# The transformed tokens of two batches in one ring buffer instead of one buffer per batch

## Chip, cores and metric

One core of a Trainium2 chip (trn2). The metric is the device time of one execution in microseconds; lower is better. The tables give medians.

## The reference

A global filter along the sequence, then a feed-forward layer with exact Gelu. There are 8 batches of 3008 tokens of width 256, and the feed-forward layer is 2048 wide.

```python
X = np.fft.rfft(x, axis=1)                          # x: (8, 3008, 256)
Y = X * (filt_r + 1j * filt_i)[None]
t = np.fft.irfft(Y, n=3008, axis=1).reshape(24064, 256)
h = t @ w_in                                        # (24064, 2048)
out = (0.5 * h * (1 + erf(h / sqrt(2)))) @ w_out    # (24064, 256)
```

## The kernel before

The transform is done in four stages of matmuls. The last of them, `s4`, leaves the tokens of one batch transposed in SBUF, in a tile `y` of its own (two such tiles in turn). The feed-forward part walks over all 24,064 tokens in 47 chunks of 512, whatever batch they belong to. As 3008 is not a multiple of 512, a chunk can hold the end of one batch and the start of the next. `segs` then cuts it in two, and each piece needs its own matmul and its own weight load.

```python
def s4(self, b, grp, half, both=False):
    if grp == 0 and half == 0:
        self.y[b] = self.py.tile([128, 2, 3072], BF16, tag="y", name="y_sb")   # py: 2 buffers
    # ... four matmuls into ps ...                                  (L306)
    self._evac(yv, pv, both, 1.0 / self.S)     # into y[b]: L221 on DVE, some L217 on ACT

def segs(self, t):
    lo, hi, r = t * TCH, (t + 1) * TCH, []
    while lo < hi:
        b = lo // self.S
        n = min(hi, (b + 1) * self.S) - lo
        r.append((b, lo - b * self.S, n))
        lo += n
    return r

def mm1(self, t, jc):                          # one of 16 blocks of 128 columns of w_in
    # ...
    for b, off, n in self.segs(t):
        for dc in range(2):
            nc.tensor.matmul(ps[:, o:o + n], lhsT=self.w_in_sb[:, dc, jc * 128:jc * 128 + 128],
                             rhs=self.y[b][:, dc, off:off + n], ...)             # L407
        o += n
    nc.scalar.activation(out=self.st["g", t][:, jc, :], in_=ps, func=AF.Gelu)   # L410
```

The stages of the next batch are mixed into the feed-forward part slot by slot. A slot is one `mm1` of a chunk (two matmuls of 512 columns) and one `mm2` of the chunk before it (four matmuls of 256 columns, L421). `hi` is the first slot of the chunk in which the next batch begins:

```python
s1, n1, r1, s2, n2, r2, s4, n4 = hi - 94, 1, hi - 78, hi - 69, 3.7, hi - 23, hi - 17, 1
# s1: first stage (L232). r2: read back of the third stage's result from DRAM into d_sb. s4: last stage (L306)
```

So the reads of `d_sb` are issued 6 slots before the first L306 that needs them.

## Time and profile before

| | before |
|---|---|
| median of the 6 runs beside the changed kernel | 793.72 us (793.10 to 794.52) |
| the profiled run | 792.14 us, span 790.4 us |
| PE busy | 96% of the span, 90% of the chain that ended last |
| weight loads of the first matmul (L407) | 1728, of which 224 from split chunks |

In the profile's lines PE is TensorE with its matmuls, PEld the loading of TensorE's weights, ACT ScalarE, DVE VectorE and POOL GpSimd; L407 is line 407 of the kernel, and `ps_h<-y_sb,w_in_sb` says which tile is written from which.

The main lines of the page are in the prediction below. Two views more, of the kernel before: the waits of PE, and the waits of PE's weight loads. The columns are the line that waited, what for, the sum in us, how many times, and the longest.

```profile
PE ps_c L322 <- DMA x_sb<-in_x_dram: 10.3, 4, 6.2
...
PE ps_s L306 <- DMA d_sb<-R: 2.0, 5, 0.8
```

```profile
PEld L306 <- DMA d_sb<-R: 2.9, 4, 1.3
...
PEld L306 <- issue: 2.1, 3, 0.8
```

The matmul and its weight load wait side by side, so the two sums overlap and must not be added. PE waits for DMA at the start (x, and then the filters, which show in the chain), and now and then for `d_sb` before the last transform stage.

### The profile page before, as it was taken

To read this page: it belongs to the slowest core of one execution; us is meant where nothing else is said; L and a number is where in the kernel's file an instruction comes from. 1 tells how busy PE (TensorE), PEld (TensorE's weight loads), DVE (VectorE), ACT (ScalarE), POOL (GpSimd) and SP (SyncE) were. 2 spreads that over 40 slices of the span, in tenths; PEclk is the share of its full clock that TensorE was granted. 3 is DMA by queue.
4 is the path that set the end of the run, shared out by engine and by line. 5 is a ranking of instruction groups with operands and counts; after the bars stand their busy time and mean duration, and the time that the engine had idled before them with its cause. 6 is when DMAs were issued, how large, how long until landed. Compare 5 with 4: busy or idle time off the path is not lost.

```text
span 790.4 us, 14879 instructions
## 1 busy us (share of the span) xinstructions
PE 762.5 (96%) x5950; PEld 545.3 (69%) x6042; DVE 407.4 (52%) x733; ACT 570.1 (72%) x982; POOL 65.3 (8%) x161
## 2 busy tenths in 40 slices
PE   4799999999999999999999999999999999999997
PEld 4656776666676767767677677777767676676666
DVE  7794766466463645646455564536545376411011
ACT  6688965798557985588755887568965788566663
POOL 8610200011000100002000010001100000000000
PEclk9999999999999999999999999999999999999999
DMA  8994862565434653446614466154642521501111
GB/s 125 187 163 134 152 157 68 147 123 117 107 87 153 107 136 88 105 136 132 147 45 120 140 116 158 48 170 94 130 121 74 154 80 54 134 31 37 41 41 54
DMA packets 88390, 87.23 MB, mean 110 GB/s; under 512 B 6080, under 2 KB 78272, under 8 KB 88320
## 3 DMA queue, kind: packets, MB, share of 16 engines
q1 hardware_dynamic: 77760, 68.70, 30.6%
q0 software_dynamic: 10560, 17.57, 15.6%
q8 instruction: 47, 0.77, 0.4%
q14 instruction: 23, 0.19, 0.1%
HBM read 57.15 MB, written 46.66 MB: 131 GB/s over the span
## 4 chain that ended last, share of the span: by engine, by line
PE 90%; DMA 4%; POOL 2%; DVE 2%; issue 1%; ACT 0%; SPq 0%; DVEq 0%; POOLq 0%
PE ps_o L421 41%; PE ps_h L407 37%; PE ps_s L232 3%; PE ps_s L306 3%; PE ps_s L279 2%; PE ps_s L255 2%; DMA d_sb<-R 2%; DMA F<-in_filt_i_dram 1%; POOL F L95 1%; DMA x_sb<-in_x_dram 1%; DVE d_sb L219 1%; POOL x_sb L87 1%; DVE p L352 0%; DVE y_sb L221 0%; POOL kap L457 0%
## 5 line engine op out<-in xcount | busy, mean ns | idle before, releaser
L410 ACT ACTIVATE g_sb<-ps_h 128x512 bf16<-128x512 f32 x752 | 439.1, 596 | 190.2 <-PE ps_h L407 166.0
L421 PE MATMUL ps_o<-w_out_sb,g_sb 128*128 128x256 bf16 x3008 | 449.1, 272 | 2.6
L407 PE MATMUL ps_h<-y_sb,w_in_sb 128*128 128x512 bf16 (+7 forms) x1636 | 428.1, 350 | 0.2 <-ACT y_sb L217 0.2
L421 PEld LDWEIGHTS <-g_sb 128*128 128x128 bf16 x3008 | 287.7, 98 | 128.3
L407 PEld LDWEIGHTS <-w_in_sb 128*128 128x128 bf16 x1728 | 164.9, 98 | 27.1 <-issue 0.5
L425 DVE COPY ost<-ps_o 128x512 f32<-128x512 f32 x94 | 64.4, 685 | 125.2 <-PE ps_o L421 124.7
L262 DVE TENSOR_TENSOR p<-ps_s,F 128x512 bf16<-128x512 f32 x84 | 58.1, 692 | 103.5 <-ACT p L261 97.0
L221 DVE TENSOR_SCALAR y_sb<-ps_s 128x376 bf16<-128x376 f32 x120 | 65.3, 548 | 82.4 <-PE ps_s L306 82.4
L219 DVE CAST a_sb<-ps_s 96x512 bf16<-96x512 f32 x112 | 76.3, 686 | 41.0 <-PE ps_s L232 40.9
L219 DVE CAST v_sb<-ps_s 128x512 bf16<-128x512 f32 x84 | 57.6, 687 | 12.9 <-PE ps_s L279 12.9
L306 PEld LDWEIGHTS <-d_sb 96*128 96x128 bf16 x512 | 33.8, 97 | 30.7 <-DMA d_sb<-R 2.9
L260 ACT ACTIVATE p<-ps_s 64x512 bf16<-64x512 f32 x84 | 49.8, 593 | 2.1 <-ACT g_sb L410 0.2
L261 ACT CAST p<-ps_s 64x512 bf16<-64x512 f32 x84 | 48.5, 577 | 1.0
L100 POOL COPY gate<-p 1x1 bf16<-1x1 bf16 x48 | 8.5, 176 | 479.8 <-DVE p L264 479.8
L232 PE MATMUL ps_s<-x_sb,T 94*96 94x512 bf16 x112 | 42.9, 383 | 0.4
L306 PE MATMUL ps_s<-T,d_sb 96*128 96x94 bf16 x448 | 36.3, 204 | 3.1 <-DMA d_sb<-R 2.0
L264 DVE TENSOR_TENSOR p<-p,p 128x512 bf16<-128x512 bf16 x84 | 35.7, 425 | 2.9
L87 POOL DMA_DIRECT2D x_sb<-in_x_dram x64 | 33.9, 530 | 19.3 <-issue 11.0
L263 DVE TENSOR_TENSOR p<-p,F 128x512 bf16<-128x512 bf16 x84 | 34.9, 415 | 0.0
L279 PE MATMUL ps_s<-p,T 128*128 128x256 bf16 x168 | 32.1, 273 | 0.4
L255 PE MATMUL ps_s<-b_sb,T 128*128 128x256 bf16 x168 | 32.1, 273 | 0.4
L279 PEld LDWEIGHTS <-T 128*128 128x128 bf16 x168 | 16.4, 98 | 20.0 <-DVE p L264 0.5
(84 smaller groups left out, 188.4 us busy)
## 6 DMA issues: line engine op xcount, KB each, us to landing
out_dram<-ost SPq DMA_DIRECT2D x94, 256.0 KB, 2.6
x_sb<-in_x_dram POOLq DMA_DIRECT2D x64, 188.0 KB, 4.0
R<-a_sb SPq DMA_DIRECT2D x56, 192.0 KB, 3.0
b_sb<-R SPq DMA_DIRECT2D x28, 384.0 KB, 4.3
R<-v_sb SPq DMA_DIRECT2D x42, 256.0 KB, 4.0
d_sb<-R SPq DMA_DIRECT2D x56, 192.0 KB, 4.5
w_in_sb<-in_moe_w_in_dram POOLq DMA_DIRECT2D x2, 512.0 KB, 8.9
w_out_sb<-in_moe_w_out_dram POOLq DMA_DIRECT2D x2, 512.0 KB, 9.6
```

Source lines behind the costliest of these rows:

```text
L219: self.nc.vector.tensor_copy(out=out, in_=in_)
L221: self.nc.vector.tensor_scalar(out=out, in0=in_, scalar1=scale, scalar2=None, op0=ALU.mult)
L232: nc.tensor.matmul(ps[0:96, :], lhsT=self.T1, rhs=self.st[b, "x"][:, 2 * u:2 * u + 2, :], start=True, stop=True)
L260: nc.scalar.activation(out=p2[0:64], in_=ps[64:128], func=AF.Copy, scale=-1.0)
L261: nc.scalar.copy(out=p2[64:128], in_=ps[0:64])
L262: nc.vector.tensor_tensor(out=p1, in0=ps, in1=f(0), op=ALU.mult)
L279: nc.tensor.matmul(ps[:, 256 * i:256 * i + 256], lhsT=self.T3[:, k].rearrange("p a b -> p (a b)"), rhs=w[:, 256 * i:256 * i + 256], start= ...
L306: nc.tensor.matmul(ps[:, 94 * i:94 * i + 94], lhsT=d[:, (grp % 2) * 4 + i, 128 * half:128 * half + 128], rhs=t4, start=True, stop=True)
L407: nc.tensor.matmul(ps[:, o:o + n], lhsT=self.w_in_sb[:, dc, jc * 128:jc * 128 + 128], rhs=self.y[b][:, dc, off:off + n], start=(dc == 0), ...
L410: nc.scalar.activation(out=self.st["g", t][:, jc, :], in_=ps, func=AF.Gelu)
L421: nc.tensor.matmul(ps[:, tile_i % 2, :], lhsT=g[:, jc, tile_i * 128:tile_i * 128 + 128], rhs=self.w_out_sb[:, jc, :], start=(jc == 0), sto ...
L425: nc.vector.tensor_copy(out=ost, in_=ps)
```

## The change

Its intent: boundaries between batches 0|1, 2|3, 4|5 and 6|7 no longer split a chunk, because two batches lie one behind the other in one buffer of 6016 tokens. Only the boundaries where the ring wraps (batches 2, 4 and 6) still do. The three scratch arrays of the table set-up share that one buffer before the tokens need it.

```diff
--- before.py
+++ after.py
@@ -48,7 +48,7 @@
         self.pd = pool("pd", 4)
         self.pool = pool
         self.po = pool("po", 3)
-        self.py = pool("py", 2)
+        self.py = pool("py", 1)
         self.pg = pool("pg", 2)
         self.small = pool("small", 1)
         self.dram = pool("dram", 2, space=bass.MemoryType.DRAM)
@@ -156,8 +156,7 @@
         v.tensor_copy(out=ri, in_=ri_i)
         ts(out=n2, in0=n2, scalar1=1.0 / self.S, scalar2=None, op0=ALU.mult)
         ts(out=ri, in0=ri, scalar1=-0.25, scalar2=0.25, op0=ALU.mult, op1=ALU.add)
-        wr = self.py.tile([128, 2, K1, NB], FP32, tag="y", name="wr")
-        w, r = wr[:, 0], wr[:, 1]
+        w, r = self.gen[:, 1], self.gen[:, 2]
         ts(out=w, in0=self.kap, scalar1=n2, scalar2=ri, op0=ALU.mult, op1=ALU.add)
         ts(out=r, in0=w, scalar1=RND, scalar2=-RND, op0=ALU.add, op1=ALU.add)
         v.tensor_tensor(out=w, in0=w, in1=r, op=ALU.subtract)
@@ -296,9 +295,10 @@
 
     def s4(self, b, grp, half, both=False):
         nc = self.nc
-        if grp == 0 and half == 0:
-            self.y[b] = self.py.tile([128, 2, 3072], BF16, tag="y", name="y_sb")
-        y = self.y[b]
+        if b == 0 and grp == 0 and half == 0:
+
+            self.ring = self.py.tile([128, 2, 2 * self.S], BF16, tag="y", name="y_sb")
+        o = b % 2 * self.S
         d = self.st[b, "d", grp // 2]
         ps = self.bank("ps_s4", both)
         t4 = (self.T4 if b else self.T4c).rearrange("p a b -> p (a b)")
@@ -306,7 +306,7 @@
             nc.tensor.matmul(ps[:, 94 * i:94 * i + 94],
                              lhsT=d[:, (grp % 2) * 4 + i, 128 * half:128 * half + 128],
                              rhs=t4, start=True, stop=True)
-        yv = y[:, half, 0:self.S].rearrange("c (m w) -> c m w", w=HB)[:, :, 4 * grp:4 * grp + 4]
+        yv = self.ring[:, half, o:o + self.S].rearrange("c (m w) -> c m w", w=HB)[:, :, 4 * grp:4 * grp + 4]
         pv = ps[:, 0:376].rearrange("c (i m) -> c m i", i=4)
         self._evac(yv, pv, both, 1.0 / self.S)
 
@@ -388,11 +388,10 @@
 
 
     def segs(self, t):
-        lo, hi, r = t * TCH, (t + 1) * TCH, []
+        lo, hi, r, m = t * TCH, (t + 1) * TCH, [], 2 * self.S
         while lo < hi:
-            b = lo // self.S
-            n = min(hi, (b + 1) * self.S) - lo
-            r.append((b, lo - b * self.S, n))
+            n = min(hi, (lo // m + 1) * m) - lo
+            r.append((lo % m, n))
             lo += n
         return r
 
@@ -402,10 +401,10 @@
             self.st["g", t] = self.pg.tile([128, 16, TCH], BF16, tag="g", name="g_sb")
         ps = self.ps_h.tile([128, TCH], FP32, tag="h", name="ps_h")
         o = 0
-        for b, off, n in self.segs(t):
+        for off, n in self.segs(t):
             for dc in range(2):
                 nc.tensor.matmul(ps[:, o:o + n], lhsT=self.w_in_sb[:, dc, jc * 128:jc * 128 + 128],
-                                 rhs=self.y[b][:, dc, off:off + n], start=(dc == 0), stop=(dc == 1))
+                                 rhs=self.ring[:, dc, off:off + n], start=(dc == 0), stop=(dc == 1))
             o += n
         nc.scalar.activation(out=self.st["g", t][:, jc, :], in_=ps, func=AF.Gelu)
 
@@ -452,7 +451,8 @@
                           in_=m.T1.rearrange("p (h r k) -> p k h r", h=2, r=2))
     m.load_x(0, 1, 2)
     m.pi = m.iota(g, "pi", [128, 1], [[0, 1]], cm=1, dt=I32)
-    m.kap = m.py.tile([128, K1, 2 * NB], FP32, tag="y", name="kap")[:, :, 0:NB]
+    m.gen = m.py.tile([128, 3, K1, NB], FP32, tag="y", name="gen")
+    m.kap = m.gen[:, 0]
     for sgn, lo in ((1, 0), (-1, 32)):
         nc.gpsimd.iota(m.kap[:, :, lo:lo + 32], pattern=[[1, K1], [sgn * NA, 32]], base=min(0, sgn * NA),
                        channel_multiplier=0, allow_small_or_imprecise_dtypes=True)
```

## The prediction

> **What bounds the kernel now.** I read the page first: the busy shares, then the chain that ended last, then the costly groups.
>
> ```profile
> PE 762.5 (96%) x5950; PEld 545.3 (69%) x6042; DVE 407.4 (52%) x733; ACT 570.1 (72%) x982; POOL 65.3 (8%) x161
> ...
> PE 90%; DMA 4%; POOL 2%; DVE 2%; issue 1%; ACT 0%; SPq 0%; DVEq 0%; POOLq 0%
> ...
> L421 PE MATMUL ps_o<-w_out_sb,g_sb 128*128 128x256 bf16 x3008 | 449.1, 272 | 2.6
> L407 PE MATMUL ps_h<-y_sb,w_in_sb 128*128 128x512 bf16 (+7 forms) x1636 | 428.1, 350 | 0.2 <-ACT y_sb L217 0.2
> L421 PEld LDWEIGHTS <-g_sb 128*128 128x128 bf16 x3008 | 287.7, 98 | 128.3
> L407 PEld LDWEIGHTS <-w_in_sb 128*128 128x128 bf16 x1728 | 164.9, 98 | 27.1 <-issue 0.5
> ```
>
> PE is busy 96% of the span and is 90% of the chain, so whatever leaves PE's queue should shorten the time, one for one. The change touches only the first matmul of the feed-forward part (L407). Its weight loads are 1728. Without splits there would be 47 chunks x 16 column blocks x 2 halves of the depth = 1504. The other 224 are 7 batch boundaries x 32. (Of the matmuls themselves only 1636 records are left in the trace, so I count by the loads.)
>
> The mean durations are a trap. In the groups kept apart by shape, a 512-column matmul of L407 is 379 ns, a 448-column one 353 and a 64-column one 193. So a pair of pieces seems to cost 167 ns more than a whole. But consecutive matmuls overlap, and these ends are modelled. What counts is the spacing of starts. I therefore looked at the timeline of ACT, where one Gelu (L410) marks each slot (one slot is two first matmuls and four second ones of 256 columns, plus what is mixed in). Four stretches: chunk 41, split 64/448 with nothing mixed in; chunk 42, not split, nothing mixed in; chunk 5, split 448/64 with one transform matmul (L232) per slot; chunk 17, split 320/192, also with L232. In each line the first number is the start.
>
> ```profile
> 703.79 0.60 ACT L410 ACTIVATE g_sb<-ps_h 128x512 bf16<-128x512 f32 x1 [0.28 <-PE ps_h L407]
> 704.66 0.60 ACT L410 ACTIVATE g_sb<-ps_h 128x512 bf16<-128x512 f32 x1 [0.28 <-PE ps_h L407]
> 705.54 0.60 ACT L410 ACTIVATE g_sb<-ps_h 128x512 bf16<-128x512 f32 x1 [0.28 <-PE ps_h L407]
> 706.41 0.60 ACT L410 ACTIVATE g_sb<-ps_h 128x512 bf16<-128x512 f32 x1 [0.28 <-PE ps_h L407]
> ```
>
> ```profile
> 717.72 0.60 ACT L410 ACTIVATE g_sb<-ps_h 128x512 bf16<-128x512 f32 x1 [0.27 <-PE ps_h L407]
> 718.59 0.60 ACT L410 ACTIVATE g_sb<-ps_h 128x512 bf16<-128x512 f32 x1 [0.27 <-PE ps_h L407]
> 719.45 0.60 ACT L410 ACTIVATE g_sb<-ps_h 128x512 bf16<-128x512 f32 x1 [0.27 <-PE ps_h L407]
> 720.32 0.60 ACT L410 ACTIVATE g_sb<-ps_h 128x512 bf16<-128x512 f32 x1 [0.27 <-PE ps_h L407]
> ```
>
> ```profile
> 129.59 0.60 ACT L410 ACTIVATE g_sb<-ps_h 128x512 bf16<-128x512 f32 x1 [0.51 <-PE ps_h L407]
> 130.69 0.60 ACT L410 ACTIVATE g_sb<-ps_h 128x512 bf16<-128x512 f32 x1 [0.51 <-PE ps_h L407]
> 131.80 0.60 ACT L410 ACTIVATE g_sb<-ps_h 128x512 bf16<-128x512 f32 x1 [0.51 <-PE ps_h L407]
> 132.91 0.60 ACT L410 ACTIVATE g_sb<-ps_h 128x512 bf16<-128x512 f32 x1 [0.51 <-PE ps_h L407]
> ```
>
> ```profile
> 324.91 0.60 ACT L410 ACTIVATE g_sb<-ps_h 128x512 bf16<-128x512 f32 x1 [0.50 <-PE ps_h L407]
> 326.00 0.60 ACT L410 ACTIVATE g_sb<-ps_h 128x512 bf16<-128x512 f32 x1 [0.50 <-PE ps_h L407]
> ```
>
> The split slot of chunk 41 takes about 0.873 us and the whole slot of chunk 42 about 0.868. ACT waits for PE ahead of every Gelu, so this spacing is PE's. With the trace's nanoseconds averaged over 14 slots: chunk 41 873.5, chunk 42 868.5, chunk 5 1106.7, chunk 17 1093.5.
>
> **What the Trainium skill says.** "TensorE: Matmul & The Clock Gate", section "Back-to-back issue gap", gives for the full clock N/2.4 + 2.5 ns between starts: 215.8 ns for 512 columns, 109.2 for 256, with the 2.5 ns a fixed cost per matmul. A slot of two and four comes to 868.3; the trace has 868.5. By the same formula a split adds two fixed costs, 5.0 ns a slot; chunk 41 shows 5.0. The same section also gives a sustained 131 ns per 512-column matmul in streams of loads and matmuls; this trace doesn't have that. The section "LDWEIGHTS (loading the stationary operand)" puts a load at its columns over 1.2 GHz, 107 ns for 128; the trace has 98. If loads were not hidden, chunk 41 would have shown two loads more per slot, about 196 ns; it shows 5. The page "Perfetto Trace Analysis", section "Identifying the Most-Contended Engine", warns that matmul busy time is a poor measure because matmuls are pipelined; the 379 ns durations against 216 ns spacings agree.
>
> **The change part by part.**
> First, splits removed. The ring holds two batches, 6016 tokens, so only boundaries 2, 4 and 6 remain split. Boundaries 1, 3, 5 and 7 lie in chunks 5, 17, 29 and 41 and become whole: 4 x 32 = 128 matmuls and 128 loads less. The order of the built program agrees: 12,086 rows on PE before, 11,830 after.
> - Chunk 41: 16 slots x 5.0 ns = 0.08 us (its 16 slots took 13.968 us, those of chunk 42 13.893: 0.075).
> - Chunks 17 and 29: a transform matmul is mixed in. Its slot cost comes from chunk 0, where a slot is two first matmuls and one L232: 651.8 ns; less 2 x 215.8 that leaves 220. So an unsplit slot with it is 868.5 + 220 = 1088.5 and the split one 1093.5: again 5.0. Two chunks x 16 x 5.0 = 0.16 us.
> - Chunk 5: 1106.7 - 1088.5 = 18 ns a slot, in 14 slots. The reason may be that two short matmuls of 64 columns come last and the load for L232 behind them (123 ns, 94 rows by 96 columns, against 98 for the usual one) isn't hidden under them. Chunk 41, where the short pieces come first and an L421 load follows long ones, has no such excess. 14 x 18 + 2 x 5 = 0.26 us.
> Sum: 0.08 + 0.16 + 0.26 = 0.50 us, all on PE and on the path.
>
> Second, waits moved. A joined chunk reads both batches in one matmul, so it has to wait for the last write of the new batch before its first matmul, where before the old batch's piece could start without it. In the built program the wait for DVE stands on the first LDWEIGHTS of these four chunks. In the trace before, the last L221 write of batch 1 ends 1.03 us ahead of the first load of chunk 5; for the batches 3, 5 and 7 it is 1.32 us. So this wait costs nothing, unless DVE is pushed back by a microsecond.
>
> Third, the table work at the start. The three scratch arrays move into one tile, and the frequencies become contiguous. L161 read them with gaps in 1.08 us, against 0.96 us for the similar L162 without: 0.1 us at best on DVE. But there the chain is the loads of x and of the filters (DMA of the filters and its issue on POOL are the largest part of the chain in the first 50 us). 0 us. The instruction counts of DVE, ACT, POOL and SP are unchanged, and so is what is transferred.
>
> **The rivals.**
> A: one tile for two batches makes false dependences. If a read of the old batch waited for each write of the new one, each of the 16 slots with an L306 group would hold PE for an eviction, some 0.55 us (L221: 548 ns each) and a hop. 7 batches x 16 x 0.5 us = 56 us, over 840 us in all. In favour: there is one buffer where two were. Against: in the built program L407 has the same 750 waits for ACT, and 15 for DVE before and after (four now on a LDWEIGHTS), so the dependences are kept by range and none was added. The evictions of L221 carry only their 120 waits for PE in both. I hold this at about 1%.
>
> B: the busy durations are real costs. 128 loads x 98 ns = 12.5 us, or 32 x (167 + 166 + 166 + 167) ns = 21 us from the durations of the shapes; the time would be 773 to 781, and the larger one just over 2% faster. In favour: PE is the bound and its busy time will fall by that much. Against: chunks 41 and 42 differ by 0.075 us, where this would want 3 to 5. About 1%.
>
> C: the gain drowns in waits that vary. In the last slot before the L306 groups start, the chunks 9, 15, 21, 27, 33 and 39 stretch to between 1.04 and 2.01 us, waiting for the second transform's reads back from DRAM (d_sb). Over the smallest, 1.04, that is 2.8 us in sum in this one run, from 0 to 0.97 each. It differs from batch to batch with the same program, so it will differ from run to run, and by more than 0.5 us. The three runs before span 1.36 us. This is my main case for the size of the visible difference: the traces may differ by 0.5 us plus or minus 1.
>
> **Range and chances.** 793.73 - 0.50 = 793.2 us. The uncertainty is that of rival C: about 0.8 us either way for a median of a few runs, some more if the layout shifts DMA phases. I take 792.0 to 794.5. Faster by over 2% would need rival B, slower by over 2% rival A: 1% each. 98% within 2%.
>
> **What would show it right or wrong.** L407 should have 1600 weight loads, and no shapes of 448 or 64 columns; 192 and 320 columns also vanish, while 384/128 and 256 stay. The Gelu starts of chunk 41 should come every 0.8685 us, those of chunk 17 every 1.0885 and of chunk 5 every 1.0885 (1.107 before); chunks 11, 23 and 35 keep 1.0935. PE busy time should fall by more than the span does, since the modelled durations overlap. L407 should show no wait for DVE at the head of chunks 5, 17, 29 and 41. The remaining difference in span should lie in the waits for d_sb. I would be wrong if a wait of L407 for y appeared with several hundred ns a time, if the start of the first L407 (49.2 us) moved by more than a microsecond, or if the chunks that were joined shortened by 2 us or more each.

## The result and the profile after

| | before | changed |
|---|---|---|
| median of 6 runs | 793.72 us (793.10 to 794.52) | 791.91 us (790.64 to 793.63) |
| ratio | | 0.9978, 95% interval 0.9965 to 0.9991 |
| span of the profiled run | 790.4 us | 790.6 us |

Within 2%, as forecast, but 0.1 us under the lower end of the range of 792.0 to 794.5, and the difference of 1.8 us is more than three times the 0.5 us forecast. And yet the span of the profiled run is 0.2 us longer, not shorter. So the two traces cannot show a gain of 1.8 us; they show what a single run is made of. In the changed kernel most lines bear a number one lower: L407, L410, L421 and L232 of before are L406, L409, L420 and L231 (L306 stays). First the page of the changed kernel, beside the lines that the prediction quotes of before:

```profile
PE 762.5 (96%) x5817; PEld 539.1 (68%) x5914; DVE 407.6 (52%) x733; ACT 570.5 (72%) x982; POOL 65.3 (8%) x161
...
L406 PE MATMUL ps_h<-y_sb,w_in_sb 128*128 128x512 bf16 (+2 forms) x1503 | 426.6, 365 | 0.2 <-ACT y_sb L216 0.2
L406 PEld LDWEIGHTS <-w_in_sb 128*128 128x128 bf16 x1600 | 155.1, 98 | 23.0 <-issue 0.5
```

The loads of the first matmul (now L406) fell from 1728 to 1600 and their busy time by 9.8 us, while PE's busy time stayed at 762.5. Almost 10 us of this line's weight-load time left the trace and PE is as busy as before.

Then the slots. In the timeline of ACT each Gelu (now L409) marks one slot of PE, and the first column is its start. Chunk 41 of the changed kernel, whole now:

```profile
704.06 0.60 ACT L409 ACTIVATE g_sb<-ps_h 128x512 bf16<-128x512 f32 x1 [0.27 <-PE ps_h L406]
704.93 0.60 ACT L409 ACTIVATE g_sb<-ps_h 128x512 bf16<-128x512 f32 x1 [0.27 <-PE ps_h L406]
705.80 0.60 ACT L409 ACTIVATE g_sb<-ps_h 128x512 bf16<-128x512 f32 x1 [0.27 <-PE ps_h L406]
706.66 0.60 ACT L409 ACTIVATE g_sb<-ps_h 128x512 bf16<-128x512 f32 x1 [0.27 <-PE ps_h L406]
```

And chunk 5, whole now, with the first transform stage mixed in:

```profile
130.38 0.60 ACT L409 ACTIVATE g_sb<-ps_h 128x512 bf16<-128x512 f32 x1 [0.49 <-PE ps_h L406]
131.47 0.60 ACT L409 ACTIVATE g_sb<-ps_h 128x512 bf16<-128x512 f32 x1 [0.49 <-PE ps_s L231]
132.56 0.60 ACT L409 ACTIVATE g_sb<-ps_h 128x512 bf16<-128x512 f32 x1 [0.49 <-PE ps_h L406]
133.65 0.60 ACT L409 ACTIVATE g_sb<-ps_h 128x512 bf16<-128x512 f32 x1 [0.49 <-PE ps_h L406]
```

The spacing in chunk 41 went from 0.873 to 0.868 us, that in chunk 5 from 1.107 to 1.09. From the trace's nanoseconds, averaged over 14 slots: chunk 41 from 873.4 to 868.4, chunks 17 and 29 from 1093.3 to 1088.4, chunk 5 from 1106.6 to 1088.4. The waits of the changed kernel for the reads back:

```profile
PE ps_s L306 <- DMA d_sb<-R: 1.3, 3, 0.6
```

```profile
PEld L306 <- DMA d_sb<-R: 2.3, 3, 1.0
```

To see the whole, I split each trace by the first Gelu of each chunk. (The time of a chunk is from its first Gelu to the first Gelu of the next. The six chunks "before L306" are 9, 15, 21, 27, 33 and 39, whose last slot waits for the first reads of `d_sb`.)

| us | before | changed | difference |
|---|---|---|---|
| from the start to the first Gelu | 49.90 | 50.85 | +0.96 |
| chunks 5, 17, 29, 41 (the joined ones) | 65.96 | 65.47 | -0.49 |
| the six chunks before L306 | 89.22 | 88.84 | -0.38 |
| the other 37 chunks | 585.29 | 585.44 | +0.15 |
| span | 790.36 | 790.60 | +0.24 |

The joined chunks show the forecast: 17.459, 17.269, 17.268 and 13.968 us became 17.193, 17.193, 17.194 and 13.893. The rest is in places that the change doesn't touch. The start came 0.96 us later, where the chain goes through the loads of x and the filters. Single chunks before L306 moved from -0.72 (chunk 39) to +0.65 us (chunk 27) with nothing changed in their programs.

So the question for the experiments: is the missing 1.3 us of the timed gain (1.8 - 0.5) chance in these DMA waits, or something that the new layout brings and that a single pair of traces can't show?

- **Theory N:** the change is worth the 0.5 us in four chunks, and the rest is noise, of the before side too.
- **Theory L:** the layout (ring, merged scratch) systematically shortens the start or the DMA waits by a microsecond.
- **Theory S:** the splits themselves were worth 1.8 us and the trace misleads.

### The profile page after: what moved, and what is told of

The parts are those of the page before. It is cut to its first block, busy times and chain, and to the rows that moved or that the text cites. A ratio compares the mean times of both kernels' runs of the same rounds, so it can differ in the third digit from the quotient of the medians.

```text
span 790.6 us, 14618 instructions
## 1 busy us (share of the span) xinstructions
PE 762.5 (96%) x5817; PEld 539.1 (68%) x5914; DVE 407.6 (52%) x733; ACT 570.5 (72%) x982; POOL 65.3 (8%) x161
## 4 chain that ended last, share of the span: by engine, by line
PE 90%; DMA 5%; DVE 2%; POOL 1%; issue 1%; ACT 0%; SPq 0%; DVEq 0%; POOLq 0%
PE ps_o L420 41%; PE ps_h L406 37%; PE ps_s L231 3%; PE ps_s L306 3%; PE ps_s L278 2%; PE ps_s L254 2%; DMA d_sb<-R 1%; DMA F<-in_filt_i_dram 1%; DMA F<-in_filt_r_dram 1%; DMA x_sb<-in_x_dram 1%; DVE d_sb L218 1%; POOL x_sb L87 1%; POOL F L95 1%; DMA R<-a_sb 1%; DMA b_sb<-R 0%
## 5 line engine op out<-in xcount | busy, mean ns | idle before, releaser
L409 ACT ACTIVATE g_sb<-ps_h 128x512 bf16<-128x512 f32 x752 | 439.4, 597 | 189.1 <-PE ps_h L406 163.5
L420 PE MATMUL ps_o<-w_out_sb,g_sb 128*128 128x256 bf16 x3008 | 449.0, 272 | 3.0
L406 PE MATMUL ps_h<-y_sb,w_in_sb 128*128 128x512 bf16 (+2 forms) x1503 | 426.6, 365 | 0.2 <-ACT y_sb L216 0.2
L420 PEld LDWEIGHTS <-g_sb 128*128 128x128 bf16 x3008 | 287.6, 98 | 133.7
L406 PEld LDWEIGHTS <-w_in_sb 128*128 128x128 bf16 x1600 | 155.1, 98 | 23.0 <-issue 0.5
L306 PEld LDWEIGHTS <-d_sb 96*128 96x128 bf16 x512 | 33.8, 97 | 30.2 <-issue 2.3
L259 ACT ACTIVATE p<-ps_s 64x512 bf16<-64x512 f32 x84 | 49.9, 594 | 2.2 <-ACT g_sb L409 0.2
L231 PE MATMUL ps_s<-x_sb,T 94*96 94x512 bf16 x112 | 42.6, 381 | 0.5
L306 PE MATMUL ps_s<-T,d_sb 96*128 96x94 bf16 x448 | 36.3, 204 | 2.6 <-DMA d_sb<-R 1.3
```

What stands on the lines that cost most here:

```text
L231: nc.tensor.matmul(ps[0:96, :], lhsT=self.T1, rhs=self.st[b, "x"][:, 2 * u:2 * u + 2, :], start=True, stop=True)
L259: nc.scalar.activation(out=p2[0:64], in_=ps[64:128], func=AF.Copy, scale=-1.0)
L306: nc.tensor.matmul(ps[:, 94 * i:94 * i + 94], lhsT=d[:, (grp % 2) * 4 + i, 128 * half:128 * half + 128], rhs=t4, start=True, stop=True)
L420: nc.tensor.matmul(ps[:, tile_i % 2, :], lhsT=g[:, jc, tile_i * 128:tile_i * 128 + 128], rhs=self.w_out_sb[:, jc, :], start=(jc == 0), sto ...
```

## Experiments

### The kernel before against itself, and the changed kernel again

No edit in either. The kernel before stood at 792.12 us (11 runs, 790.80 to 793.98).

> The kernel before, unchanged, timed against itself: how far two equal kernels come apart. Theory N (the change is worth the 0.5 us of PE work of the four joined chunks, and the other 1.2 us of the measured 1.8 is chance in the DMA waits): ratio within 0.9985 to 1.0015, and the intervals of such comparisons wide enough for 1 us. Theory L (the new layout itself brings more than a microsecond): this run shows a ratio within 0.9995 to 1.0005, noise too small for the missing 1.2 us.

Measured: 793.43 us, ratio **1.0012** (0.9998 to 1.0027), between equal programs. Its span is 1.67 us longer than in the first trace of the same kernel; the first Gelu alone came 1.94 us later (51.84 instead of 49.90 us). The joined chunks are 65.965 us against 65.964. Theory L's bound for the noise (0.9995 to 1.0005) was missed: 0.9 us between equal kernels is possible with this many runs.

> The changed kernel again. Theory N: the ratio moves towards 0.9994 (0.5 us), anywhere in 0.998 to 1.0005. Theory L: 0.9978 again, within 0.0007. Both: in its trace the chunks 5, 17, 29 and 41 take 17.19, 17.19, 17.19 and 13.89 us, as in the first trace of it; all other differences from the trace before lie at the first L406 and in the chunks that wait for the reads back (9, 15, 21, 27, 33, 39).

Measured: 791.75 us, ratio **0.9994** (0.9980 to 1.0008). In the trace the four chunks take 17.194, 17.194, 17.193 and 13.893 us. The changed kernel hardly moved from the first measurement (791.91); it is the kernel before that came out 1.6 us lower than before (792.12 after 793.72). That suggests that most of the first difference was on the before side, but doesn't prove it: `before_again`, the same program in the same rounds, stood at 793.43. Theory N's band holds the ratio; theory L's 0.9978 lies just outside the interval. Pooled (12 changed runs against 23 of the kernel before), the difference of the means is -1.1 us plus or minus 0.7, which holds the forecast 0.5. My expectation on where differences lie was not complete: chunk 4, before the L306 of batch 1, was off by 0.34 us too, with a wait of the same kind.

### The ring with all boundaries split

```diff
-            n = min(hi, (lo // m + 1) * m) - lo
+            n = min(hi, (lo // self.S + 1) * self.S) - lo
```

The layout of the change with PE's instructions of before.

> The ring and the merged scratch of the change, but each batch boundary still split, so PE has all the matmuls of before. Theory N: ratio 1.000 within the noise (0.9985 to 1.0015). Theory L: 0.9984, 1.3 us faster than before, as only the 0.5 us of the matmuls is given up. Theory S (the splits alone were worth 1.8 us, the trace misleads): 1.000, while the changed kernel of the same rounds is at 0.9978.

Measured: 792.75 us, ratio **1.0007** (0.9992 to 1.0022). Theory L's 0.9984 is outside the interval. At most some 0.6 us of gain is left to the ring (the lower end of the interval, 0.9992). The four boundary chunks are 65.962 us, as in the kernel before: the ring alone removes nothing there. The six chunks before L306 do not settle it: they take 89.22 and 88.97 us in the two traces of the kernel before, and 88.84, 88.07 and 87.89 us in the three with the ring (`after`, `after_again` and this run). They are shorter in all three, but that is three traces against two, and it isn't in the timed runs of this kernel. Theory S is not excluded by this run, but it wanted the changed kernel at 0.9978 in these rounds, which came out at 0.9994.

### Splits by the dozen

If one split slot costs so little, many of them should still add up to little. The edit, in the changed kernel (`lo + 256` in the first, `lo + 448` in the second, `lo + (64 if lo == t * TCH else TCH)` in the third):

```diff
-            n = min(hi, (lo // m + 1) * m) - lo
+            n = min(hi, lo + 256, (lo // m + 1) * m) - lo
```

> The changed kernel with each chunk cut in two halves of 256 tokens: 46 chunks x 32 more matmuls and loads (44 whole ones become two, the boundaries 384/128 and 128/384 become three; 256/256 stays). If a split slot costs 5.0 ns: 46 x 16 x 5.0 = 3.7 us slower than the changed kernel of these rounds, plain slots 873.5 ns apart. Theory S: the four chunks of the change would have been worth 1.8/4 = 0.45 us each, so 46 x 0.45 = 21 us. If each load cost its 98 ns: 46 x 32 x 98 ns = 144 us.

Measured: 796.39 us, ratio 1.0050 (1.0037 to 1.0064); 4.6 us above the changed kernel of the same rounds where 3.7 was expected. The difference of the spans is 5.3, but 1.1 of that is the first Gelu and 1.5 the chunks before L306. (These 1.5 hold 0.5 for the splits in these chunks.) The slots themselves are as expected. Chunk 42 of this kernel, in ACT's timeline:

```profile
718.12 0.60 ACT L409 ACTIVATE g_sb<-ps_h 128x512 bf16<-128x512 f32 x1 [0.28 <-PE ps_h L406]
718.99 0.60 ACT L409 ACTIVATE g_sb<-ps_h 128x512 bf16<-128x512 f32 x1 [0.28 <-PE ps_h L406]
719.87 0.60 ACT L409 ACTIVATE g_sb<-ps_h 128x512 bf16<-128x512 f32 x1 [0.28 <-PE ps_h L406]
720.74 0.60 ACT L409 ACTIVATE g_sb<-ps_h 128x512 bf16<-128x512 f32 x1 [0.28 <-PE ps_h L406]
```

0.873 us a slot (873.4 by the nanoseconds), and 80 ns more per chunk in nearly all chunks. Theory S wanted 21 us for the 1472 extra pairs of a load and a matmul (46 x 32), unhidden loads 144 us. Both are refuted.

The next two ask why the slots of chunk 5 cost 18 ns and not 5.

> The changed kernel with each chunk cut into 448 and 64 tokens, the short piece last. It tests why the slots of chunk 5 cost 18 ns and not 5. Theory W (the slow weight load of L232, 123 ns, is not hidden under the two short matmuls): plain slots 873.5 ns apart, as with 64/448; only slots with L232 mixed in reach 1107. Rival (any load behind two short matmuls is exposed): plain slots at some 882 to 887 as well. Time in all by theory W: 44 whole chunks x 16 x 5.0 = 3.5 us and some 90 slots with L232 x 13 ns = 1.2 us, 4.7 us over the changed kernel; by the rival about 12 us over it.

Measured: 795.86 us, ratio 1.0033 (1.0017 to 1.0050). Plain slots (chunks 41 and 42) 873.4 ns; slots with the first transform stage in chunks 5, 17 and 29, 1106.7. So the slots are as theory W wrote them. The sum is not: 4.7 us over the changed kernel was expected, and it is 2.8 us over the kernel before by the medians (the changed kernel wasn't in these rounds). In the traces, all chunks but the six before L306 take 3.7 us more than in the changed kernel. One part of the miss is a count: only some 60 slots (in chunks 0, 5, 17 and 29) have the first stage behind a 64-column piece, not 90. Chunk 17 of this kernel, split 448/64:

```profile
324.34 0.60 ACT L409 ACTIVATE g_sb<-ps_h 128x512 bf16<-128x512 f32 x1 [0.51 <-PE ps_h L406]
325.44 0.60 ACT L409 ACTIVATE g_sb<-ps_h 128x512 bf16<-128x512 f32 x1 [0.51 <-PE ps_h L406]
326.55 0.60 ACT L409 ACTIVATE g_sb<-ps_h 128x512 bf16<-128x512 f32 x1 [0.51 <-PE ps_h L406]
327.66 0.60 ACT L409 ACTIVATE g_sb<-ps_h 128x512 bf16<-128x512 f32 x1 [0.51 <-PE ps_h L406]
```

> The changed kernel with each chunk cut into 64 and 448 tokens, the short piece first. Theory W: the short pieces stand behind the long matmuls of L421's line and ahead of long ones, so no slot costs more than 5 ns, with L232 or without: plain slots 873.5, slots with L232 1093.5. Rival (short pieces cost 18 ns anywhere beside L232): 1107 with L232.

Measured: 798.12 us, ratio 1.0064 (1.0045 to 1.0082). Plain slots 873.4, slots with the first stage 1093.4, in the same chunk 17, split 64/448:

```profile
323.67 0.60 ACT L409 ACTIVATE g_sb<-ps_h 128x512 bf16<-128x512 f32 x1 [0.50 <-PE ps_h L406]
324.76 0.60 ACT L409 ACTIVATE g_sb<-ps_h 128x512 bf16<-128x512 f32 x1 [0.50 <-PE ps_h L406]
325.86 0.60 ACT L409 ACTIVATE g_sb<-ps_h 128x512 bf16<-128x512 f32 x1 [0.50 <-PE ps_h L406]
326.95 0.60 ACT L409 ACTIVATE g_sb<-ps_h 128x512 bf16<-128x512 f32 x1 [0.50 <-PE ps_h L406]
```

1.106 and 1.093 us a slot: with the same pieces in the other order the 13 ns are gone. So the dear case is a short last piece directly ahead of the first stage's weight load. The same two traces narrow it: in the slots with L306, whose load (96 rows by 128 columns) takes 97 ns, both orders cost the same, 1043 ns a slot in chunk 10. So having fewer than 128 rows isn't enough to make a load dear. That it is the 123 ns of L232's load, and not its 96 columns in another way, fits but wasn't isolated. The times in all are the wrong way round: this kernel should be some 0.8 us faster than the one before it (60 slots x 13 ns; 1.2 us by the count in the expectation), and is 2.3 us slower by the medians. In the traces its joined and other chunks are indeed faster (654.03 against 654.62 us), but its six chunks before L306 take 91.37 us instead of 89.12; chunks 27 and 33 are 1.21 and 1.84 us over the smallest of the first trace. Why the waits are longer in this kernel is left open.

### The waits for the reads back taken away

The noise of the DMA waits should go if the reads have more time. The last stage stays where it was; all the others of batches 2 to 7 move two slots earlier, and with them the loads of the next batch's x that are tied to the second stage:

```diff
-            s1, n1, r1, s2, n2, r2, s4, n4 = hi - 94, 1, hi - 78, hi - 69, 3.7, hi - 23, hi - 17, 1
+            s1, n1, r1, s2, n2, r2, s4, n4 = hi - 96, 1, hi - 80, hi - 71, 3.7, hi - 25, hi - 17, 1
```

> The kernel before with the transforms of the batches 2 to 7 two slots (1.7 us) earlier, all but the last one (L306), so that the reads back of d_sb have two slots more. If the stretching of the chunks 9, 15, 21, 27, 33 and 39 (2.7 us over their smallest in the first trace) is the wait for these reads, it vanishes there, the sum of waits of L306 for d_sb falls under 0.5 us, and the time falls by 2 to 3 us against the kernel before. If the reads are slow because of what runs beside them, the wait only moves: same time. In both the four boundary chunks keep 17.46, 17.27, 17.27 and 13.97 us, if nothing new is mixed into them; L232 now stands in their slots 0 to 15.

Measured: 790.28 us, ratio **0.9965** (0.9950 to 0.9979) against the kernel before (793.05 in these rounds). The waits of L306 for `d_sb` no longer appear among PE's own, and one is left among the loads (in batch 1, whose schedule wasn't moved):

```profile
PEld L306 <- DMA d_sb<-R: 0.3, 1, 0.3
```

The six chunks before L306 are now equal to within 1 ns (14.888 to 14.889 us each), where they differed by up to 0.97 us. Their sum did not fall (89.33 against 89.22 us), because the shift also moves other transform work across the borders of chunks. The last slot of each shows the waits alone: 1.038 or 1.039 us in all six, against 1.04 to 2.01 us in the first trace. That the reads were late, and that their waits made these chunks vary, is thus shown. The gain of 2.8 us is what the first trace had as the sum over its smallest. The spread from run to run did not go with the waits: the six runs lie between 789.38 and 792.33 us, 2.95 us apart.

> The same shift in the changed kernel. Theory N: 0.5 us under the shifted kernel before (ratio against it 0.9994), in its trace again in the chunks 5, 17, 29 and 41 alone, 0.5 us in sum; and faster than both kernels of the study by 2 to 3 us if the waits vanish. Theory L (the layout brings a microsecond more, in waits for d_sb): as there are no such waits left, the difference between the two shifted kernels shrinks from 1.8 to 0.5 too, so this pair can't exclude L, but the waits of the two traces show it.

Measured: 789.20 us, ratio **0.9949** (0.9935 to 0.9963). It is 1.1 us under the shifted kernel before, by the medians. The waits of its loads:

```profile
PEld L306 <- DMA d_sb<-R: 0.4, 1, 0.4
```

In the two shifted traces the six chunks take 89.330 us in both, and the four boundary chunks 65.964 and 65.473: the 0.491 us again. As these timed runs still vary at the start, I ran the pair once more, with the ring and all splits beside them, on the same chip. The 12 runs of the kernel before that the ratios of this call rest on are the 11 of the call before and one new one, so they are no second base.

> The shifted kernel before once more, in the same rounds as the two below; with the waits for d_sb gone only the start (filters loaded) should still vary. It serves as the base of this call. In the trace: waits of L306 for d_sb under 0.5 us in sum again, boundary chunks 65.96 us in sum.

Measured: 790.03 us, ratio 0.9961 (0.9947 to 0.9975). One wait of 0.5 us for `d_sb` among the loads, in chunk 4 (batch 1, not moved); boundary chunks 65.963 us.

> Ring and merged scratch with all boundaries split, in the shifted schedule. Theory N: equal to the shifted kernel before within 0.5 us either way, boundary chunks 65.96 us in the trace. Theory L (the layout brings more than the splits): over 0.5 us faster than the shifted kernel before, and nearer to the shifted changed kernel.

Measured: 790.13 us, ratio 0.9966 (0.9950 to 0.9981); boundary chunks 65.964 us. It is not faster than the shifted kernel before. Its trace has one stray wait of 1.0 us for another read back (`b_sb`, in chunk 36), which shows that the second stage's reads can be late too.

> The shifted changed kernel once more. Theory N: 0.5 us under both of the above, so 0.0 to 1.0 us with this noise; boundary chunks 65.47 us in the trace. Theory L: over 1 us under the shifted kernel before and only 0.5 under the ring with all splits.

Measured: 789.78 us, ratio 0.9953 (0.9939 to 0.9967), 0.25 us under the shifted kernel before by the medians. One wait of 0.6 us for `d_sb` among the loads, again in chunk 4; boundary chunks 65.473 us.

As means with a 95% interval of twice the standard error: shifted changed kernel against shifted kernel before (12 runs each), -0.9 us plus or minus 0.6; ring with all splits (6 runs) against shifted kernel before, +0.3 plus or minus 1.0. The first interval holds 0.5 and 1.3 alike, so timing alone doesn't settle a few tenths. The second leaves no room for 1.3 us that the ring would bring at the start or elsewhere. A gain in the waits for `d_sb` it can't test, as these are gone from both sides; for that part only the ring with all splits in the old schedule speaks, which was not faster than the kernel before.

The shifted changed kernel is the fastest: 789.20 and 789.78 us, with the kernel before at 793.05 and 793.02 (nearly the same runs) beside it.

## Why the prediction was wrong, point by point

- **What bounds the kernel; durations are a trap.** Right. The modelled durations and the 98 ns of a load suggested 12 to 21 us; the joined chunks gave 0.49, and 1472 extra pairs cost 4.6 us in time, 5.0 ns a slot in the trace. One reading of the skill was loose: "Perfetto Trace Analysis" says that pipelined instructions look smaller in the trace, while here a matmul's 379 ns are longer than the spacing.
- **The sum of the change, 0.50 us.** Right in each term: 0.075 (chunk 41), 0.076 and 0.074 (17 and 29), 0.266 (5), together 0.491 in the first pair of traces and 0.491 in the shifted pair. In the ten traces without extra splits, the four chunks take 65.962 to 65.965 us with the boundaries split and 65.473 or 65.474 joined.
- **Chunk 5's 18 ns.** Right on position: a short last piece beside L232 costs 13 ns over the usual 5, elsewhere not.
- **The moved wait.** Right that it costs nothing: no wait for DVE shows at L406 in the changed trace, and the chunks that hold it are shorter.
- **The start.** The layout moved nothing that can be told from noise: the first Gelu came at 49.9, 51.8, 50.5 and 50.3 us in the four traces with the old buffers, and at 49.5 to 51.3 in the nine with the ring. The prediction's sign of being wrong, a start that moves by more than a microsecond, was no test: the same program moved by 1.94 us from one trace to the next.
- **Rivals A and B.** Refuted, as held. But in B and in the list of what would show it right I wrote that PE's busy time would fall. It did not (762.5 in both), since overlapping matmuls are counted once; only the loads' busy time fell.
- **The step that failed: "The uncertainty is that of rival C: about 0.8 us either way for a median of a few runs", laid around 793.73.** The mechanism of the gain was right; this term was mis-sized. I took it from three runs with a spread of 1.36 us. The kernel before, in all its timed runs of the later calls (on two chips), spans 790.80 to 795.16 us, 4.36 us; equal programs differed by 0.12% (0.9 us) in one comparison, and the median of the kernel before went from 793.72 to 792.12 and 793.05 between calls. Its source was also too narrow: rival C names the waits for `d_sb` alone, but the shifted kernel before, without them, still spread over 2.95 us in six runs, and the first Gelu came anywhere from 49.5 to 51.8 us in the 13 traces. The centre was bad luck too: all 35 runs of the kernel before have a mean of 793.0 us, 0.7 under the three runs. The profiled run at 792.14 was on the table and would have warned me.

What remains open: the first comparison (0.9978, 0.9965 to 0.9991) excludes 0.5 us, the second and the shifted pair do not. I hold most of its 1.8 us for chance: the changed kernel moved by 0.2 us in the next call while the kernel before moved by 1.6, and only the four chunks differ in every pair of traces by the same amount. This is argued, not shown. That the ring shortens the waits for `d_sb` in the old schedule, by up to some 0.6 us, is not excluded.

## What to carry to other kernels

Before valuing a matmul that is to be removed, look for two stretches of the same trace, one with it and one without, and take the spacing of the slots: it gave each term here to a few nanoseconds, where durations were off by a factor of 25 and more. A gain under the run-to-run spread can be shown in the trace, stage by stage, when it can't be shown in the time; and the range of a forecast must hold the spread of the side before as well, from more than three runs. The larger gain was beside the change: reads that were issued too late (two slots earlier was enough) cost 2.8 us and most of the spread between batches, though not the spread between runs.

## What the Trainium skill lacked or had wrong

- "TensorE: Matmul & The Clock Gate", section "Back-to-back issue gap": the sustained 131 ns per 512-column matmul in a stream of loads and matmuls doesn't hold here. A slot of two 512- and four 256-column matmuls takes 868.4 ns; the page's N/2.4 + 2.5, which it calls the isolated gap, gives 868.3 and so is the sustained one too, in this kernel.
- The same page, section "Part 3: Packing small matmuls — row/col tiling", says in its list of what overlaps that loads overlap with matmuls in flight only when their row groups differ. Taken alone, that doesn't hold here: full 128-row loads of 98 ns before every full matmul are hidden, and a split slot with two more of them costs 5.0 ns more. The section's text above the list also lets a load go ahead into the background weight buffer; nothing here speaks against that.
- No page read says that a 64-column last piece ahead of a load that isn't 128 columns wide (94 rows by 96 columns, 123 ns) costs more: 1106.7 ns a slot against 1093.4 with the pieces in the other order. Ahead of a 97 ns load of 96 rows by 128 columns the order made no difference (1043 ns).
